# A decode layer's forward and backward pass on one core: layer norm on another engine, earlier weight loads, and a rearranged end

## The chip, the core and the metric

The kernel runs on one core of one Trainium2 chip. A core has a matmul engine (PE, with its weight loads PEld), a vector engine (DVE), a scalar engine (ACT), a general engine (POOL) and a sync engine (SP), which run their own instruction streams and wait for each other by semaphores. Sixteen DMA engines move data between the device's memory (HBM) and the on-chip memory. Matmuls write into PSUM, which has eight banks of 512 f32 columns per partition; from there ACT or DVE copy results into the on-chip memory (an "evacuation"). The metric is device time in microseconds (us) of one execution.

## The reference

The reference is a layer of a decode step with one token, for a batch of 2, and its gradients. All inputs and outputs are bf16.

```python
xn = layernorm(x)                       # x: (2, 1, 576), eps 1e-5
out = x + A(xn) + B(xn)
# A: attention over a cache
q = xn @ wq                             # wq (576, 4096): 32 heads of 128
scores = q . k * 128**-0.5              # k_cache, v_cache (2, 16, 4096, 128); 2 query heads share a kv head
p = softmax(scores);  o = p @ v
A = o @ wo                              # wo (4096, 576)
# B: a gated product
h = (xn @ w_gate) * (xn @ w_up)         # (576, 4608) each
B = h @ w_down                          # (4608, 576)
# returned: out, and by vjp with grad_out (2, 1, 576) the gradients of
# x, k_cache, v_cache, wq, wo, w_gate, w_up, w_down
```

So every cache and weight tensor is read once (92.5 MB in all), and a gradient of the same size is written (92.5 MB). Since there is one token, nearly all gradients are outer products: the gradient of K is (dscore) x (query), of V is (probability) x (output gradient), of a weight is (input) x (output gradient).

## The kernel before, in words

**Attention.** The 16 kv heads form 4 groups of 4. The main loop (L845, `for n in range(NIT)`) has 16 steps; a step handles one batch entry and two kv heads. Each step has four *slots*: two for K heads and two for V heads. `slot` loads one head (1 MB) with SP's queue (`head_load`, L520), transposes it in two halves on DVE (`head_scores`, `t32`, L121; 1.23 us each) and multiplies it with stationary rows that hold the queries or the output gradients (16 matmuls per quarter, into a one-bank PSUM tile `ps_sc`). After the two K slots `softmax` follows, after the V slots `dscores`; `contract` then multiplies K with the score gradients and V with the probabilities (64 matmuls). POOL spreads the rows into the tiles `prm` and `dsm` (`masked`), and from these the outer products for the gradients of V and K are made.

**Outer products.** `outer_units` gives 8 units for V and 8 for K per step. A unit makes 8 matmuls into `ps_o`, a PSUM tile of two banks (two such tiles exist, tag "o"), and one evacuation of 128x1024 to a bf16 tile `so`. Four units fill an `so` tile of 1 MB, and POOL's queue stores it (L585). The list `outs` holds the units; `more(2)` takes two of them at two places in a slot. `evac` chooses the engine: it keeps an account of assumed times for DVE and ACT (`load`) and gives each evacuation to the one that would be done first by the account. DVE's account also has its transposes, so ACT gets 232 of the 256 `so` evacuations.

**Gated product.** It is cut into 9 slices of 512 columns. `mlp_units` gives 8 groups per slice: `loads` (SP, into `wgu` and `wd`), then `gate_up` with `down`, `grads` with `back`, two groups for the gradient of `w_down`, two for `w_gate` and `w_up`, and `outer_tail`. The list `side` holds the groups, and `other(per)` takes `per` of them at the end of each slot, where `per` is a quarter of the list, rounded up.

**Back of a group.** `back_units` makes, when a group's eight heads are done, the output projection (`first`: 40 matmuls with `wo`, sixteen transposes into `R`, and the rows for the next step), the gradient through `wq` (`second`), and the gradients of `wo` (`outer_o`, evacuated as `sto`) and `wq` (`outer_q`, as `stq` and `stqt`). For the last group these run after the loop.

**Buffers.** Loaded tiles (`kv`, `wgu`, `wd`, `wq`, `wo`) share 12 buffers (tag "nat"); store tiles (`so`, `sto`, `stq`, ...) share 5 (tag "st"). SP's queue issues in order, so a load that waits for a buffer holds back the loads behind it.

**Start and end.** The start loads `x` and `grad_out`, makes the layer norm on DVE (L168 to L188), constant tables, and zeroed tiles on POOL (L216 to L238). The end (`final_units`) transposes the accumulated output (`output`), collects the gradient of the normalized input (`rows`) and sends it through the layer norm on DVE (`gradient`, L817 to L833).

**Order of work.** The program order in each engine is made by a scheduler from the source order, the priorities set in `Block`, and its own estimate of when operands are ready. So an instruction need not stand where the source has it.

Of the kernel before, what the change touches and what calls it, by code (L numbers as in the profile page):

```python
# [13 lines left out]
P = 128  # L14
# [9 lines left out]
def kernel(  # L24
# [55 lines left out]
    def ps_o():  # L80
        return ps.tile([P, 2, 512], FP32, tag="o", bufs=2, name="ps_o")

    class Block:

# [19 lines left out]
    def evac(out, in_, cols):  # L104
        cv = 0.16 + cols * 0.00104
        cs = 0.19 + cols * 0.00083
        if load["v"] + cv < load["s"] + cs:
            load["v"] += cv
            nc.vector.tensor_copy(out=out, in_=in_)  # L109
        else:  # L110
            load["s"] += cs
            nc.scalar.copy(out, in_)  # L112

    def dve(us):
        load["v"] += us
# [41 lines left out]
    for be in range(4):  # L157
# [9 lines left out]
    x_f = sb.tile([2, D], FP32, tag="X", bufs=3, name="x_f")  # L167
    nc.vector.tensor_copy(x_f[:], x_bf[:])  # L168

    mu = const.tile([2, 1], FP32, name="mu")  # L170
    nc.vector.reduce_sum(mu[:], x_f[:], axis=AX.X)
    nc.vector.tensor_scalar(mu[:], mu[:], 1.0 / D, None, op0=ALU.mult)
    xn_f = sb.tile([2, D], FP32, tag="nat", bufs=12, name="xn_f")
    nc.vector.tensor_scalar(xn_f[:], x_f[:], mu[:], None, op0=ALU.subtract)
    xsq = sb.tile([2, D], FP32, tag="X", bufs=3, name="xsq")
    var = const.tile([2, 1], FP32, name="var")
    nc.vector.tensor_tensor_reduce(
        out=xsq[:], in0=xn_f[:], in1=xn_f[:], scale=1.0 / D, scalar=0.0,
        op0=ALU.mult, op1=ALU.add, accum_out=var[:],
    )  # L180
    eps_t = const.tile([2, 1], FP32, name="eps_t")
    nc.vector.memset(eps_t[:], EPS)
    rstd = const.tile([2, 1], FP32, name="rstd")
    nc.scalar.activation(rstd[:], var[:], AF.Sqrt, bias=eps_t[:], scale=1.0)
    nc.vector.reciprocal(rstd[:], rstd[:])
    nc.vector.tensor_scalar(xn_f[:], xn_f[:], rstd[:], None, op0=ALU.mult)
    xn_bf = sb.tile([2, D], BF16, tag="st", bufs=5, name="xn_bf")
    nc.vector.tensor_copy(xn_bf[:], xn_f[:])  # L188

# [25 lines left out]
    Wdy = const.tile([P, NB, 2, P], BF16, name="Wdy")  # L215
    nc.gpsimd.memset(Wdy[:], 0.0)  # L216
    dyT = sb.tile([P, 2 * NB, 32], BF16, tag="X", bufs=3, name="dyT")
# [6 lines left out]
    dM = const.tile([P, 2, 2, P], BF16, name="dM")  # L224
    for t in range(2):
        nc.gpsimd.memset(W[t][:], 0.0)
    nc.gpsimd.memset(dM[:], 0.0)
    Wms = [const.tile([P, 35, 8], BF16, name=f"Wm{i}") for i in range(2)]
# [339 lines left out]
    def outer_units(rows, bd, b, l0, oview):  # L568
        m = {}

        def unit(x, ch, A):
            def f():
                if ch == 0 and A == 0:
                    m["st"] = stile([P, 4, 8, Dh], "so")
                st = m["st"]
                o = ps_o()
                with Block() as mm:
                    for c in range(4):
                        for aa in range(2):
                            a = 2 * A + aa  # L580
                            mm(o[:, aa, c * Dh:(c + 1) * Dh], lhsT=rows[32 * a:32 * a + 32, 4 * ch + c, :],
                                             rhs=bd[32 * a:32 * a + 32, x * Dh:(x + 1) * Dh], start=True, stop=True)
                evac(st[:, 2 * A:2 * A + 2, 4 * ch:4 * ch + 4, :].rearrange("p a c d -> p a (c d)"), o[:], 1024)
                if ch == 1 and A == 1:
# [56 lines left out]
    def back_units(st):  # L641
        g, wq, wo, oT = st["g"], st["wq"], st["wo"], st["oT"]
        n0 = g * GH * Dh
        m = {}

        def first():
            yp = ps_m([P, 5, 2])
            with Block() as mm:
                for dc in range(5):
                    for h in range(GH):  # L650
                        mm(yp[:, dc, :], lhsT=wo[:, h, DOFF[dc]:DOFF[dc] + P], rhs=oT[:, 0, h, 0:2],
                                         start=(h == 0), stop=(h == GH - 1))
            nc.vector.tensor_add(acc[:], acc[:], yp[:])

            rp = ps_m([P, 2, 2, P], BF16)
            for t in range(2):
                for h in range(GH):
                    a = h // 2
                    nc.tensor.transpose(rp[32 * a:32 * a + 32, t, h % 2, :], oT[:, t, h, :], ident[:])
            m["R"] = R = sb.tile([P, 2, 2, P], BF16, tag="R", bufs=1, name="R")  # L660
            nc.vector.tensor_copy(R[:], rp[:])
            rp = ps_m([P, 32, 2])
# [4 lines left out]
            m["W"] = stationaries(rp[:], lambda h: (P * h, [[1, P]]))  # L667
            dve(0.2 + 0.5)

# [3 lines left out]
        def outer_q(k, A):  # L673
            def f():
                R = m["R"]
                if A == 0:
                    m["st"] = swtile([P, 2, GH * P], "stq")
                st = m["st"]
                o = ps_o()
                with Block() as mm:  # L680
                    for dc in range(2):
                        for aa in range(2):
                            a = 2 * A + aa
                            d0 = (2 * k + dc) * P
                            mm(o[:, aa, 256 * dc:256 * dc + 256], lhsT=xnr[32 * a:32 * a + 32, d0:d0 + P],
                                             rhs=R[32 * a:32 * a + 32, 1].rearrange("p h d -> p (h d)"),
                                             start=True, stop=True)
                evac(view(st[:], 0, P, 512 * A, [[256, 2], [GH * P, 2], [1, 256]]),
                     o[:].rearrange("p a (d n) -> p a d n", d=2), 1024)
                if A == 1:  # L690
# [17 lines left out]
        def outer_o(A, h2, k):  # L708
            def f():
                R = m["R"]  # L710
                if h2 == 0 and k == 0:
                    m["so"] = swtile([P, 4, D], "sto")
                o = ps_o()
                with Block() as mm:
                    for aa in range(2):
                        a = 2 * A + aa
                        mm(o[:, aa, 0:HD2], lhsT=R[32 * a:32 * a + 32, 0, h2, :],
                                         rhs=dyr[32 * a:32 * a + 32, k * HD2:(k + 1) * HD2], start=True, stop=True)
                evac(view(m["so"][:], 0, P, h2 * D + k * HD2, [[2 * D, 2], [1, HD2]]), o[:, :, 0:HD2], D)
                if h2 == 1 and k == 1:  # L720
# [3 lines left out]

        return [[first], [second], [outer_o(0, 0, 0), outer_o(0, 0, 1)], [outer_o(0, 1, 0), outer_o(0, 1, 1)],
                [outer_o(1, 0, 0), outer_o(1, 0, 1)], [outer_o(1, 1, 0), outer_o(1, 1, 1)],
# [6 lines left out]
    def more(n):  # L733
        for _ in range(min(n, len(outs))):
            outs.pop(0)()

    def other(n):
        for _ in range(min(n, len(side))):
            for f in side.pop(0):
                f()  # L740

    def slot(src, t, b, l, s_ps, per, mid=None):
# [102 lines left out]
    for n in range(NIT):  # L845
        g, b, s = step(n)
        l0 = G * g + 2 * s
        if len(side) < 5 and nslice < NFS:
            side += mlp_units(nslice)
            nslice += 1  # L850
        per = max(1, -(-len(side) // 4))
        new = n + 1 < NIT and step(n + 1)[0] != g
# [32 lines left out]
        if new:  # L885
            st = nxt
    end_of_K(*last[:5])
    outs += outer_units(last[5], last[6], last[1], G * last[0]["g"] + 2 * last[2], okview)
    units = back_units(last[0])
    side += final[:1] + units[:2] + final[1:] + units[2:]  # L890
    while outs or side:
# [32 lines left out]
```

## Time and profile before

| | |
|---|---|
| median of 13 runs | 521.72 us (515.55 to 530.07) |
| the profiled execution | 515.92 us, span of its instructions 514.2 us |
| busy, of the span | PE 81%, PEld 65%, DVE 69%, ACT 64%, POOL 40% |
| mean granted PE clock | 0.851 of full |
| DMA | 186.26 MB, mean 362 GB/s |
| chain that ended last | PE 44%, ACT 18%, DVE 16%, DMA 10%, issue 9%, POOL 2% |
| evacuation of 128x1024 | ACT 1.02 us, DVE 1.20 us |
| DMA issue to landing, 1 MB | K 13.1 us, V 9.7 us, `so` 10.2 us (medians) |

How to read it: "busy" is the time in which an engine executed instructions; matmuls overlap, so a busy PE is not at its peak. The DMA share is the mean busy share of the sixteen DMA engines in a stretch of time; because of rounding at the packets' ends it can stand a little above 1. "Issue" in the chain is time for which the profile shows no wait. The granted clock is the share of its full clock that PE was given.

### The profile page before, as it was taken

The numbers are of one execution on the slowest core, as the hardware profiler recorded it, in microseconds if no ns is written. First come the engines' busy times: TensorE is split into PE (matmuls) and PEld (weight loads), VectorE is DVE, ScalarE is ACT, GpSimd is POOL, SyncE is SP. The second block draws the span as 40 slices with busy tenths as digits, with TensorE's granted clock in tenths as the row PEclk, the third lists the DMA queues.
The fourth block names the chain that finished last, engine by engine and source line by source line (L and its number), as shares of the span: only waits on it lengthen the run. The fifth ranks groups of instructions, "written<-read, shape, count | busy, mean of one in ns | idle before, by whom it ended". The sixth has DMA issues, their size and how long they took to land.

```text
span 514.2 us, 20063 instructions
## 1 busy us (share of the span) xinstructions
PE 416.6 (81%) x8921; PEld 332.6 (65%) x8921; DVE 356.5 (69%) x624; ACT 327.6 (64%) x454; POOL 206.2 (40%) x372
## 2 busy tenths in 40 slices
PE   1677897978897978988889879879889878799872
PEld 0576675766786756776767757757667657677630
DVE  7687866468648948376686578749694849598464
ACT  1134797658657575676576764757777656788653
POOL 6133353332632534443343525354334255453313
PEclk9989999589859778687787896979997999999655
DMA  7997999999999999999999999999999999976656
GB/s 250 398 390 293 384 383 401 391 412 400 373 400 357 348 352 416 319 408 358 353 400 327 399 416 403 373 392 418 388 417 364 420 416 396 384 280 235 249 193 237
DMA packets 52911, 186.26 MB, mean 362 GB/s; under 512 B 4140, under 2 KB 19128, under 8 KB 44632
## 3 DMA queue, kind: packets, MB, share of 16 engines
q1 hardware_dynamic: 28392, 92.49, 48.1%
q0 software_dynamic: 24432, 92.48, 45.4%
q8 instruction: 70, 1.15, 0.9%
q14 instruction: 17, 0.14, 0.1%
HBM read 92.48 MB, written 92.48 MB: 360 GB/s over the span
## 4 chain that ended last, share of the span: by engine, by line
PE 44%; ACT 18%; DVE 16%; DMA 10%; issue 9%; POOL 2%; POOLq 0%; DVEq 0%; ACTq 0%
PE ps_sc L93 16%; ACT so L112 15%; PE ps_o L93 12%; PE ps_m L93 11%; DVE X L121 5%; DMA kv<-in_A_k_cache_dram 3%; DMA out_dram<-so 3%; DVE so L109 2%; DMA wd<-in_B_w_down_dram 2%; PE ps_m L558 1%; DMA out_dram<-stqt 1%; DVE Xd L121 1%; ACT stw L112 1%; DVE Xw L121 1%; DVE stw L109 1%
## 5 line engine op out<-in xcount | busy, mean ns | idle before, releaser
L112 ACT CAST so<-ps_o 128x1024 bf16<-128x1024 f32 x232 | 225.6, 1024 | 63.3 <-PE ps_o L93 59.9
L121 DVE STREAM_TRANSPOSE X<-kv 128x1024 f32<-128x1024 f32 x128 | 157.4, 1233 | 51.7 <-PE ps_sc L93 45.9
L93 PE MATMUL ps_sc<-X,W 128*128 128x128 bf16 x2048 | 157.2, 234 | 16.1 <-issue 9.1
L93 PEld LDWEIGHTS <-W 128*128 128x128 bf16 x2048 | 139.4, 105 | 24.3 <-issue 17.6
L585 POOL DMA_DIRECT2D out_dram<-so x64 | 49.9, 780 | 121.0 <-ACT so L112 75.2
L93 PE MATMUL ps_o<-bd,dsm 32*128 32x128 bf16 x1024 | 48.4, 233 | 14.2 <-ACT so L112 8.8
L93 PE MATMUL ps_o<-bd,prm 32*128 32x128 bf16 x1024 | 45.6, 232 | 12.2 <-ACT so L112 5.0
L93 PEld LDWEIGHTS <-dsm 32*128 32x128 bf16 x1024 | 29.3, 99 | 29.0 <-issue 22.7
L93 PE MATMUL ps_m<-kv,rowT 128*32 128x128 bf16 x2048 | 43.2, 248 | 5.1 <-issue 4.3
L93 PEld LDWEIGHTS <-prm 32*128 32x128 bf16 x1024 | 27.4, 98 | 25.3 <-issue 18.4
L93 PEld LDWEIGHTS <-rowT 128*32 128x32 bf16 x2048 | 36.2, 111 | 8.1 <-issue 5.8
L112 ACT CAST stw<-ps_o 128x1024 bf16<-128x1024 f32 x28 | 28.1, 1024 | 19.6 <-PE ps_o L93 17.3
L496 POOL COPY W<-rep 32x16 bf16<-32x16 bf16 x128 | 24.9, 195 | 31.3 <-PE ps_sc L93 23.6
L564 POOL TENSOR_TENSOR prm<-pr,maskc 128x1024 bf16<-128x1024 bf16 x16 | 30.3, 1892 | 12.3 <-DVE pr L612 12.2
L564 POOL TENSOR_TENSOR dsm<-ds,maskc 128x1024 bf16<-128x1024 bf16 x16 | 30.3, 1894 | 8.5 <-DVE ds L632 8.0
L109 DVE CAST so<-ps_o 128x1024 bf16<-128x1024 f32 x24 | 28.7, 1195 | 3.3 <-PE ps_o L93 3.3
L396 POOL DMA_DIRECT2D out_dram<-stw x18 | 13.7, 759 | 34.3 <-ACT stw L112 16.5
L93 PEld LDWEIGHTS <-Wdy 128*128 128x128 bf16 x306 | 23.0, 114 | 4.6 <-POOL dM L503 3.1
L503 POOL COPY dM<-qd 128x128 bf16<-128x128 bf16 x32 | 9.2, 290 | 41.4 <-PE ps_m L509 27.5
L112 ACT CAST std<-ps_o 128x576 bf16<-128x576 f32 x36 | 22.2, 650 | 5.4 <-PE ps_o L93 4.2
L121 DVE STREAM_TRANSPOSE Xw<-wgu 128x1152 f32<-128x1152 f32 x18 | 24.4, 1361 | 1.8 <-PE ps_sc L93 1.7
L93 PEld LDWEIGHTS <-xnr 32*128 32x128 bf16 (+1 forms) x440 | 14.0, 103 | 16.7 <-issue 12.7
(172 smaller groups left out, 549.5 us busy)
## 6 DMA issues: line engine op xcount, KB each, us to landing
out_dram<-so POOLq DMA_DIRECT2D x64, 1024.0 KB, 10.2
kv<-in_A_k_cache_dram SPq DMA_DIRECT2D x32, 1024.0 KB, 13.1
kv<-in_A_v_cache_dram SPq DMA_DIRECT2D x32, 1024.0 KB, 9.7
out_dram<-stw POOLq DMA_DIRECT2D x18, 512.0 KB, 9.6
wd<-in_B_w_down_dram SPq DMA_DIRECT2D x9, 576.0 KB, 10.1
out_dram<-std POOLq DMA_DIRECT2D x9, 576.0 KB, 9.3
wo<-in_A_wo_dram SPq DMA_DIRECT2D x4, 1152.0 KB, 14.2
wgu<-in_B_w_gate_dram SPq DMA_DIRECT2D x9, 512.0 KB, 18.6
```

Source lines behind the costliest of these rows:

```text
L93: ins = nc.tensor.matmul(*args, **kwargs)
L109: nc.vector.tensor_copy(out=out, in_=in_)
L112: nc.scalar.copy(out, in_)
L121: nc.vector.transpose(out, in_)
L396: nc.gpsimd.dma_start(out[0:512, f0:f0 + FS].rearrange("(c p) n -> p c n", p=P), st[:])
L496: nc.gpsimd.tensor_copy(view(W[t][:], 32 * a, 32, 28 + 32 * a, [[2 * WW, 4], [WW + 2, 2], [1, 2]]), view(st["rep"][:], 32 * a, 32, t * 4 * ...
L503: nc.gpsimd.tensor_copy(view(dM[:], 0, P, t * 2 * P, [[P + 2, 2], [4, 32], [1, 2]]), view(st["qd"][:], 0, P, (2 if t == 0 else 1) * GH * 2 ...
L558: nc.tensor.matmul(t_ps[:], lhsT=o_sb[:], rhs=RV[:].rearrange("p x r -> p (x r)"), start=True, stop=True)
L564: nc.gpsimd.tensor_tensor(m[:], view(rows[:], 0, P, 0, [[0, 8], [1, P]]), view(maskc[:], 0, P, 0, [[1, 8], [0, P]]), ALU.mult)
L585: nc.gpsimd.dma_start(oview[b, :, :, l0 + x].rearrange("a m n -> m a n"), st[:].rearrange("p a c d -> p a (c d)"))
```

## The change

It has four parts.

1. *Layer norm.* Five passes over `x` go from DVE to ACT (`activation` with `accum_out`, bias or scale); DVE keeps the small (2x1) steps. Three memsets (`Wdy`, `dM`, `W[0]`) go from POOL to DVE.
2. *Groups per slot.* `per` becomes a third of the list instead of a quarter, and `other` ends after it has taken a `loads` group and takes nothing at the next slot. (In the step after a group's last one `per` is still set to a quarter once the back units are added.)
3. *Back units in smaller pieces.* `first` becomes `output`, `turn(0)`, `turn(1)` and `spread`; `R` is copied in two halves.
4. *End.* After the loop every third pair comes from the two one-bank `ps_sc` buffers, which the loop no longer needs, and is evacuated as two halves; the accounts of `evac` are set to zero; the last group's `stq` and `sto` tiles come from the 12 load buffers; and the order of the last groups changes: output projection, final output and half of `outer_o` come ahead of the last `end_of_K`.

```diff
+    def ps_pair():
+        pairs_made[0] += 1
+        if ending and pairs_made[0] % 3 == 0:
+            o = [ps.tile([P, 512], FP32, tag="sc", bufs=2, name="ps_x") for _ in range(2)]
+            return [t[:] for t in o], None
+        o = ps_o()
+        return [o[:, 0, :], o[:, 1, :]], o
...
+    def evac_pair(out, o, whole, cols, view_in=lambda t: t):
+        if whole is not None:
+            evac(out(None), view_in(whole[:]), cols)
+        else:
+            for a in range(2):
+                evac(out(a), view_in(o[a]), cols // 2)
...
-    nc.vector.tensor_copy(x_f[:], x_bf[:])
-    nc.vector.reduce_sum(mu[:], x_f[:], axis=AX.X)
+    nc.scalar.activation(x_f[:], x_bf[:], AF.Copy, accum_out=mu[:])
+    nc.vector.tensor_scalar(negmu[:], mu[:], -1.0 / D, None, op0=ALU.mult)
     nc.vector.tensor_scalar(mu[:], mu[:], 1.0 / D, None, op0=ALU.mult)
-    nc.vector.tensor_scalar(xn_f[:], x_f[:], mu[:], None, op0=ALU.subtract)
+    nc.scalar.activation(xn_f[:], x_f[:], AF.Identity, bias=negmu[:], scale=1.0)
-    nc.vector.tensor_tensor_reduce(
-        out=xsq[:], in0=xn_f[:], in1=xn_f[:], scale=1.0 / D, scalar=0.0,
-        op0=ALU.mult, op1=ALU.add, accum_out=var[:],
-    )
+    nc.scalar.activation(xsq[:], xn_f[:], AF.Square, accum_out=var[:])
-    nc.scalar.activation(rstd[:], var[:], AF.Sqrt, bias=eps_t[:], scale=1.0)
+    nc.scalar.activation(rstd[:], var[:], AF.Sqrt, bias=eps_t[:], scale=1.0 / D)
     nc.vector.reciprocal(rstd[:], rstd[:])
-    nc.vector.tensor_scalar(xn_f[:], xn_f[:], rstd[:], None, op0=ALU.mult)
-    nc.vector.tensor_copy(xn_bf[:], xn_f[:])
+    nc.scalar.activation(xn_bf[:], xn_f[:], AF.Copy, scale=rstd[:])
...
-    nc.gpsimd.memset(Wdy[:], 0.0)
+    nc.vector.memset(Wdy[:], 0.0)
...
-    for t in range(2):
-        nc.gpsimd.memset(W[t][:], 0.0)
-    nc.gpsimd.memset(dM[:], 0.0)
+    nc.vector.memset(dM[:], 0.0)
+    nc.vector.memset(W[0][:], 0.0)
+    nc.gpsimd.memset(W[1][:], 0.0)
...
+        stq = nat if g == NGRP - 1 else swtile
...
-                    m["st"] = swtile([P, 2, GH * P], "stq")
+                    m["st"] = stq([P, 2, GH * P], "stq")
...
     def other(n):
+        if waits[0]:
+            waits[0] -= 1
+            return
         for _ in range(min(n, len(side))):
-            for f in side.pop(0):
+            group = side.pop(0)
+            for f in group:
                 f()
+            if group[0].__name__ == "loads":
+                waits[0] = 1
+                return
...
-        per = max(1, -(-len(side) // 4))
+        per = max(1, -(-len(side) // 3))
...
+    ending.append(1)
+    load["v"] = load["s"] = 0.0
+    waits[0] = 0
+    units = back_units(last[0])
+    side += final[:1] + units[:1] + final[1:2] + units[3:5]
+    more(2)
     end_of_K(*last[:5])
     outs += outer_units(last[5], last[6], last[1], G * last[0]["g"] + 2 * last[2], okview)
-    units = back_units(last[0])
-    side += final[:1] + units[:2] + final[1:] + units[2:]
+    side += units[1:3] + final[2:] + units[5:]
     while outs or side:
         more(2)
         other(1)
```

The units of `outer_units`, `outer_q` and `outer_o` take their pair from `ps_pair` and hand it to `evac_pair`; outside the end both do what `ps_o` and `evac` did.

## The prediction

> **What bounds the kernel now.** I read three views in this order: stretches of the span (busy time of each engine, granted TensorE clock, DMA share, GB/s), then the instructions in order of time at both ends, then the chain of waits of the last 38 us.
>
> The stretches; columns are start:end, length, busy us (instructions) of PE, PEld, DVE, ACT, POOL, then clock, DMA share, GB/s:
>
> ```profile
> 10.00:40.00 30.00, 20.41 (x366) 17.92 (x367) 23.31 (x52) 8.16 (x11) 6.14 (x20) 0.94 1.04 390
> 40.00:50.00 10.00, 7.12 (x213) 6.05 (x210) 7.41 (x16) 3.49 (x8) 4.85 (x7) 1.00 0.73 277
> 50.00:450.00 400.00, 341.47 (x7414) 276.61 (x7415) 274.67 (x467) 273.64 (x382) 165.08 (x296) 0.85 1.00 386
> 450.00:476.00 26.00, 23.54 (x541) 18.79 (x538) 23.38 (x39) 22.49 (x32) 11.32 (x14) 1.00 0.68 258
> 476.00:514.20 38.20, 23.52 (x409) 12.86 (x397) 20.06 (x36) 18.25 (x22) 10.42 (x14) 0.55 0.61 225
> ```
>
> The reader is to see three regimes. From 50 to 450 us the DMA engines are full (share 1.00). At 40 to 50 they lose (1 - 0.73) x 10 = 2.7 us. From 450 on reading is over, and they run at 0.68 and 0.61: compute sets the end. No byte is added or removed by this change, so it can gain only in the gap at 40 to 50, in the last 38 us, and in what little the middle loses.
>
> The start, in order of time (start, duration, engine, instruction):
>
> ```profile
> 0.74 1.28 ACT L184 ACT_TABLE_LOAD   x1 [0.74 <-PEq L908]
> 0.94 0.19 DVE L245 MEMSET accx<- 128x160 f32 x1
> 2.07 2.79 DVE L168 CAST x_f<-x_bf 2x576 f32<-2x576 bf16 x1 [0.94 <-DMA x_bf<-in_A_x_dram]
> ...
> 8.88 0.45 DVE L188 CAST xn_bf<-xn_f 2x576 bf16<-2x576 f32 x1
> 9.26 0.21 DVE L130 CAST identf<-ident 128x128 f32<-128x128 bf16 x1
> ```
>
> The layer norm holds DVE from 2.07 to 9.33; only then come DVE's 2.3 us of constant tables, and at 12.81 the first matmul with real weights. The first cast took 2.79 us; the same cast at the end of the kernel takes 0.44.
>
> The chain that ended last, from 485 us on:
>
> ```profile
> 485.60 1.02 ACT so L112
> 486.62 0.04 issue
> 486.66 0.61 PE ps_o L93 x8
> ...
> 488.88 1.94 ACT so L112 x2
> 490.81 0.04 issue
> 490.86 1.23 PE ps_o L793 x5
> ...
> 493.73 2.29 PE ps_o L804 x8
> 496.02 0.56 PE ps_o L93 x8
> ```
>
> Matmuls and evacuations take turns: with two pairs of banks, PE waits for an evacuation, then the evacuation for PE.
>
> **Part 1, layer norm on ACT.** The nearest row for an ACT pass over 576 columns is `std`, 128x576, 0.65 us; the read of an accumulator after Exp took 0.19. From the landing at 2.07: cast with sum 0.84, `negmu` on DVE 0.14 and two hand-overs of about 0.05 (3.15), centering 0.65 (3.8), square with sum 0.84 (4.65), table load 1.28, since Sqrt now comes after another function set (5.9), Sqrt 0.29 and reciprocal 0.15 with hand-overs (6.5), scaling 0.65 (7.2). Before it was 9.33. In the built order DVE has its constants right behind the reciprocal, so they start at 6.55 instead of 9.26: 2.7 us earlier. Ahead of `negmu` stand three memsets moved from POOL, of 1152, 256 and 624 f32 elements per partition. At the rate of the `accx` row (0.19 us for 160, 0.07 for 10: 0.8 ns each) they take 1.8 us and end at 2.7, before the sum is there. At POOL's rows (2.02, 0.52 and half of 2.52) they would take 3.8 and delay it by 1.6. Behind the constants stand the `xs` copies, `dyr`, `xnr`, and the weight transposes. `wo` had landed by 11.4 (issue 3.11, 8.3 to landing), and its transpose moves only from 15.5 to 12.8.
>
> What is this worth? The DMA engines are full from 10 to 40 us on loads already issued; SP's next load stands at 46.65, waiting for a buffer. A start 2.7 us earlier frees it 2.7 earlier, and the gap has just 2.7 us to give. I take **2.5**, bounds 0 (another buffer turns out to be the late one) and 2.7.
>
> The first row above shows the table load at 1.28 us and work right after it. The Trainium skill ("ScalarE: Activation LUTs", What ACT_TABLE_LOAD costs) adds a drain of about 1.38 us to each switch, which speaks against this part: by it the start would gain 1.1. Here the load before Exp started 0.02 us after the copy ahead of it ended, so no drain stands in front of it.
>
> **Part 2, weight loads two slots ahead.** A slot is 7.1 us (16 steps of 4 slots from 24 to 478). Before, a slice's 8 groups went 2 to a slot, the loads one slot ahead. Now the first slot issues the loads alone, the second is skipped, and the rest goes 3 to a slot. DVE waited for a landing weight only here:
>
> ```profile
> DVE Xd L121 <- DMA wd<-in_B_w_down_dram: 6.7, 2, 3.5
> ```
>
> Both waits lie in stretches with a DMA share of 1.0, so removing them only makes later data late. What is new: `wgu` and `wd` hold 2 of the 12 load buffers 7.1 us longer, on SP's in-order queue the K and V loads stand behind them, and a slice's five stores come in two slots instead of four. Nothing shows a longer hold directly; the dearest row is the window 240 to 245, where loads of a new group and of a slice meet and the share is 0.58 (2.1 us lost). Bounds for 8 slices: gain 6.7, loss 8 x 2.1 = 17. I take **0**, by the 400 us row above: queued transfers cover delays of this size nearly everywhere.
>
> **Part 3, the end.** In the chain from 485 to 506 PE waits for evacuations, and for DVE steps of the final gradient ahead of them, about 11.6 us (1.0 + 1.9 + 1.0 + 1.0 for `so`, then 2.6, 0.7, 2.7 and 0.7). A third pair and both engines would hide these, bound 11.6. Less comes off. The scheduler leaves 19 units of `so` after the last score matmul instead of 16, which moves work and removes none. One pair in three is evacuated as two halves: ACT 2 x 0.58 (the `stqt` row, 512 columns) against 1.02. ACT's list from the last `bd` on sums to 23.6 us against 21.7. And `rows` moves back: the built PE order has the accx matmuls after 10 of the 16 `sto` matmuls, where before all 16 followed. On DVE the last two `stq` evacuations stand behind the whole gradient.
>
> So the end follows from this chain. PE's busy time from 476 on is 23.5 us, plus 3 units of about 0.6, of which 7.2 come from the accx matmuls on (2.29 for those, 6 `sto` at 0.21, 20 for `stq` at 0.18): 18.1 us lie ahead. The loop ends some 2.5 us sooner, as the 3 units left it. With about 3.5 us of waits left, accx starts at 473.5 + 18.1 + 3.5 = 495. The matmuls and gradient took 493.73 to 503.84 before, 7.2 without the four `sto` evacuations among them: 502.2. Two `stq` on DVE at 1.23: 504.7 instead of 508.5, and with the stores behind them about 510.2 instead of 514.2. I take **4.0**, bounds 0 (PE at half clock and the gradient chain eat it) and 11.6. The final `stq` and `sto` tiles in the load buffers, and `R` copied in halves, count as nothing: no row of the last 38 us waits for a store buffer, and `R` is 0.41 us.
>
> The row of 476 on shows the clock at 0.55; from 480 to 485 PE was busy 4.57 of 5 us and stayed at 0.50. The skill ("TensorE: Matmul & The Clock Gate", Part 1) lets the clock return after some 3.4 us of sustained work, and PE's 18.1 us would then be about 10 and the end 8 us earlier. These rows don't bear that out.
>
> **Sum.** The profiled execution took 515.92 us (span 514.2). 515.92 - 2.5 - 0 - 4.0 = 509.4. It is one of the fastest of the 13 runs shown; their median is 521.72, and the same 6.5 us off that gives **515.2**, the forecast. About 1% (5 us) is what can be told from no change.
>
> **Rivals.** (a) *The end does not shorten*, as the gradient chain and ACT's 23.6 us take the place of the bank waits: only 2.5 is left, 519.2. For it speaks that `stq` stands behind six microseconds of serial DVE work; against it, ACT was idle over half the last 38 us (18.25 busy). (b) *Slower: load buffers.* Held one slot longer, they let SP's queue run dry once per slice, and DMA idles where its share is now 1.00. At 1.9 us each (nearly the 240 us window), 8 slices cost 15.2: 521.7 - 6.5 + 15.2 = 530.4. It beats the gain from 0.8 us per slice, and makes the kernel slower by over 1% from 1.5. For it: SP waited 144 us in all for PE to free K and V buffers, 21 times. Against: DMA stayed full in spite of that. (c) *More*: all bank waits go (11.6), the gap closes (2.7) and the weight waits count for half (3.4): 504. (d) *It does nothing*: ACT's table load and the moved memsets eat the start, another load the gap, PE the end: 521.
>
> **Chances.** Forecast 0.52, (a) 0.18, (b) 0.15, (c) 0.10, (d) 0.05. The forecast's own range is 510 to 519. The range of 8 in 10 reaches halfway into (b) and (c): 505 to 527. Faster by over 1% (below 516.5) is (c), and about four fifths of the forecast's case: 0.52. Slower by over 1% is (b) and a little of (d): 0.17. Within 1%: 0.31.
>
> **What would show it.** Right: `xn_bf` ready near 7.2, first weight matmul near 10.1, share above 0.9 at 40 to 50, 50 to 450 still 1.00, and about 4 us less from the last score matmul to the end than the loop's shift explains. Wrong: DVE's memsets past 3 us; a middle share under 0.97 with SP waiting on `wd` or `wgu` readers (rival b); the last chain on DVE's gradient and `stq` with the same length (rival a); a granted clock of 1.0 in the last 30 us (rival c).

## The result

| | before | changed |
|---|---|---|
| median (runs) | 522.95 us (48) | 535.59 us (11) |
| lowest to highest | 515.11 to 531.25 | 527.13 to 537.93 |
| the profiled execution (span) | 515.92 us (514.2) | 535.76 us (533.9) |
| mean granted clock in the profile | 0.851 | 0.807 |

The ratio is 1.0218, interval [1.0158, 1.0278]: the change makes the kernel slower by 2.2%. The forecast was 515.2 us with a range of 505 to 527; the measured 535.59 us lies above it. Medians here and below are of all runs shown; the ratios leave disturbed runs out on both sides, so that a ratio can differ from the quotient of two medians.

The stretches of the changed kernel, with the columns of the prediction's first fence (start:end, length, busy us of PE, PEld, DVE, ACT, POOL, clock, DMA share, GB/s); the last two are cut at its own last score matmul:

```profile
10.00:40.00 30.00, 22.98 (x383) 20.25 (x383) 23.71 (x39) 7.72 (x11) 5.88 (x20) 0.83 1.04 386
40.00:50.00 10.00, 8.63 (x245) 7.25 (x243) 6.95 (x15) 6.37 (x13) 6.08 (x10) 1.00 1.01 380
50.00:450.00 400.00, 334.33 (x7003) 272.63 (x7001) 266.96 (x445) 259.98 (x358) 154.60 (x279) 0.81 0.95 365
450.00:492.00 42.00, 37.07 (x827) 30.77 (x827) 32.81 (x56) 32.25 (x46) 18.22 (x28) 0.92 0.82 308
492.00:533.90 41.90, 27.41 (x464) 15.66 (x461) 22.21 (x46) 22.17 (x33) 12.99 (x16) 0.58 0.61 226
```

The gap at 40 to 50 is closed (0.73 before, 1.01 now). The middle, full before, is not full any more: (1.00 - 0.95) x 400 = 20 us of DMA time are lost there. The two spans differ by 533.9 - 514.2 = 19.7 us. So between these two executions the middle accounts for the whole loss, and nothing of what start and end were to bring is left beside it. The execution of the kernel before is 7 us faster than its median, so 20 us is the difference of these two; by the ratio the change costs 2.18% of 522.95, 11.4 us. By hundreds of us from 50 on, the share is 0.94, 0.96, 0.92 and 0.98, against 1.02, 0.98, 1.00 and 1.00 before: it goes in several places, not in one.

The start, rows of ACT, DVE and PE in order of time (start, duration, engine, instruction; in brackets the idle time before it and what ended that):

```profile
2.07 0.68 ACT L190 ACTIVATE x_f<-x_bf 2x576 f32<-2x576 bf16 x1
...
2.66 0.19 ACT L190 ACTIVATION_READ_ACCUMULATOR x_f<-x_bf 2x1 f32 x1
2.98 0.08 DVE L191 TENSOR_SCALAR negmu<-mu 2x1 f32<-2x1 f32 x1
...
4.52 0.19 ACT L197 ACTIVATION_READ_ACCUMULATOR xsq<-xn_f 2x1 f32 x1
4.72 1.28 ACT L201 ACT_TABLE_LOAD   x1
6.02 0.29 ACT L201 ACTIVATE rstd<-var,eps_t 2x1 f32<-2x1 f32 x1
...
6.43 0.20 DVE L150 CAST identf<-ident 128x128 f32<-128x128 bf16 x1
6.53 0.78 ACT L204 ACTIVATE xn_bf<-xn_f,rstd 2x576 bf16<-2x576 f32 x1 [0.22 <-DVE rstd L202]
...
9.97 1.22 PE L105 MATMUL ps_m<-xs,wq 128*128 128x2 bf16 x40
```

DVE's constants start at 6.43 instead of 9.26, and the first matmul with real weights at 9.97 instead of 12.81: 2.8 us earlier.

Who held SP's queue on the `wd` load, by the waits from 50 to 450 us (engine, line, what it waited for: us in total, times, longest). The kernel before, whose `wd` load is L319, waited 4.9 us:

```profile
SPq L319 <- PE ps_m L93: 2.1, 1, 2.1
SPq L319 <- DVE Xw L121: 1.8, 1, 1.8
SPq L319 <- PE ps_o L93: 1.0, 1, 1.0
```

The changed kernel, where it is L335, waited 31.7 us:

```profile
SPq L335 <- DVE Xw L141: 13.3, 2, 7.4
SPq L335 <- PE ps_m L105: 12.3, 2, 6.6
SPq L335 <- PE ps_o L105: 3.4, 2, 2.7
SPq L335 <- DVE negb L619: 2.7, 1, 2.7
```

The K and V loads (L520 before, L536 in the changed kernel) waited longer, too, for the readers of weights, `Xw` on DVE. In both kernels they waited longest for matmuls of PE. The first two rows are of the kernel before, the last two of the changed kernel:

```profile
SPq L520 <- PE ps_o L93: 140.7, 20, 18.9
SPq L520 <- DVE Xw L121: 9.1, 2, 5.4
...
SPq L536 <- PE ps_o L105: 136.3, 23, 20.5
SPq L536 <- DVE Xw L141: 21.6, 3, 8.7
```

One case of a `wd` load that was held up, in SP's queue in order of time:

```profile
111.40 1.41 SPq L333 DMA_DIRECT2D wgu<-in_B_w_up_dram  x1
126.85 0.34 SPq L335 DMA_DIRECT2D wd<-in_B_w_down_dram  x1
132.30 0.34 SPq L536 DMA_DIRECT2D kv<-in_A_k_cache_dram  x1
147.42 1.18 SPq L536 DMA_DIRECT2D kv<-in_A_v_cache_dram  x2
```

`wd` is issued 15.5 us after `wgu`'s last load (6.6 in the same place before: 112.00 to 118.58), after waits of 7.4 us for `Xw` and 6.6 us for matmuls; the K load behind it follows at 132.30 (120.70 before) and the V loads at 147.42 (138.18 before). What had been queued lasts till about 140 (share 0.99 from 135 to 140), and then the engines run dry; stretches with the columns as above:

```profile
140.00:145.00 5.00, 3.37 (x73) 3.17 (x72) 4.74 (x9) 1.93 (x2) 1.64 (x8) 1.00 0.30 115
145.00:150.00 5.00, 4.44 (x179) 3.70 (x176) 2.13 (x5) 3.88 (x5) 3.56 (x6) 1.00 0.61 185
```

This gap belongs to part 2. Two of the runs below show it in the same stretch: e15_slots_end, which has part 2 without the halves of `R`, has it (first row), and e4_start_end, which has the halves without part 2, has not (second row):

```profile
140.00:145.00 5.00, 3.37 (x72) 3.17 (x71) 4.70 (x9) 1.90 (x2) 1.58 (x8) 0.99 0.31 117
...
140.00:145.00 5.00, 4.68 (x99) 3.92 (x102) 1.55 (x2) 1.97 (x3) 3.03 (x10) 0.52 0.99 377
```

The chain that ended last, from just ahead of the `accx` matmuls (PE L841) on (start, duration, engine, instruction; "issue" is time for which the profile shows no wait):

```profile
515.01 0.41 ACT sto L124
...
515.49 0.67 issue
516.16 0.32 POOL Wt L290
...
516.52 0.30 POOL Wt L290
...
517.97 2.31 PE ps_o L841 x8
...
522.89 0.44 DVE t L865
...
523.36 0.76 DVE t L866
...
524.14 0.53 DVE t L867
...
524.94 1.63 DVEq L962
526.58 1.14 DVE stq L121
```

From the last score matmul to the end it is 41.7 us, against 39.9 before. By the rows of PE 21 units of `so` are left then, against 18; the prediction, which counted 19 against 16, has the same three more.

### The profile page after: what moved, and what is told of

The parts are those of the page before. It is cut to its first block, busy times and chain, and to the rows that moved or that the text cites. A ratio compares the mean times of both kernels' runs of the same rounds, so it can differ in the third digit from the quotient of the medians.

```text
span 533.9 us, 20080 instructions
## 1 busy us (share of the span) xinstructions
PE 432.0 (81%) x8921; PEld 347.4 (65%) x8921; DVE 358.1 (67%) x628; ACT 334.5 (63%) x466; POOL 201.8 (38%) x369
## 4 chain that ended last, share of the span: by engine, by line
PE 43%; DVE 9%; ACT 9%; DMA 8%; issue 6%; POOL 1%; DVEq 0%; POOLq 0%; ACTq 0%
PE ps_sc L105 14%; PE ps_m L105 12%; PE ps_o L105 10%; ACT so L124 7%; DMA kv<-in_A_k_cache_dram 3%; DVE X L141 3%; DMA out_dram<-so 2%; DMA kv<-in_A_v_cache_dram 2%; DVE so L121 2%; PE ps_m L574 1%; ACT sto L124 1%; PE ps_m L646 1%; PE ps_m L624 1%; DVE Xw L141 1%; PE ps_m L525 1%
## 5 line engine op out<-in xcount | busy, mean ns | idle before, releaser
L124 ACT CAST so<-ps_o 128x1024 bf16<-128x1024 f32 x228 | 221.0, 1021 | 69.9 <-PE ps_o L105 61.6
L105 PE MATMUL ps_sc<-X,W 128*128 128x128 bf16 x2048 | 161.4, 239 | 7.6 <-DVE X L141 3.2
L105 PEld LDWEIGHTS <-W 128*128 128x128 bf16 x2048 | 144.4, 108 | 15.1 <-issue 7.7
L105 PE MATMUL ps_o<-bd,dsm 32*128 32x128 bf16 x1000 | 50.6, 247 | 20.1 <-ACT so L124 13.3
L105 PEld LDWEIGHTS <-dsm 32*128 32x128 bf16 x1024 | 33.2, 105 | 35.8 <-issue 31.3
L105 PE MATMUL ps_m<-kv,rowT 128*32 128x128 bf16 x2048 | 40.5, 239 | 5.8 <-issue 3.6
L105 PEld LDWEIGHTS <-prm 32*128 32x128 bf16 x1024 | 29.6, 98 | 21.7 <-issue 14.3
L105 PEld LDWEIGHTS <-rowT 128*32 128x32 bf16 x2048 | 34.0, 107 | 8.0 <-issue 4.1
L512 POOL COPY W<-rep 32x16 bf16<-32x16 bf16 x128 | 24.8, 194 | 22.9 <-PE ps_sc L105 15.2
L105 PEld LDWEIGHTS <-Wdy 128*128 128x128 bf16 x306 | 26.2, 124 | 4.9 <-DVE Xo L141 2.9
L105 PEld LDWEIGHTS <-xnr 32*128 32x128 bf16 (+1 forms) x440 | 12.6, 102 | 21.1 <-issue 16.4
L571 ACT COPY o_sb<-ps_m 128x128 f32<-128x128 f32 x32 | 8.7, 271 | 25.6 <-PE ps_m L105 25.5
```

The lines of the kernel that those rows point to most:

```text
L105: ins = nc.tensor.matmul(*args, **kwargs)
L512: nc.gpsimd.tensor_copy(view(W[t][:], 32 * a, 32, 28 + 32 * a, [[2 * WW, 4], [WW + 2, 2], [1, 2]]), view(st["rep"][:], 32 * a, 32, t * 4 * ...
L571: nc.scalar.copy(o_sb[:], o_ps[:])
```

## The experiments

In the expectations, "parts" are the four of the section on the change: 1 layer norm, 2 groups per slot, 3 smaller back units, 4 the end. "Hold" is worked out for each run from the profile's rows: from the issue of a slice's first `wgu` load to the end of the last DVE read of its weights (`Xw` of `wgu`; in e12_hold_tail the added read), on average over slices 2 to 9. The share is that of the DMA engines from 50 to 450 us of the profiled execution. Ratios are to the kernel before on the same chip, in the same set of runs; its median was 523.73 us beside e1, e2, e4 and e9, 522.22 beside e6, e8, e11 and e10_end_only, 525.24 beside e5, e12, e13 and e10_end_merged, 518.03 beside e15 and e16, and 525.15 beside e14 and e17. For e5 and e12 the quotient of the medians (1.035 and 1.048) is more than a percent above the ratio, so the size of these two losses is known no better than that. Share and hold are of one execution each; that of e8 took 546.02 us, 12 above its median.

| run | what it is | median us | ratio [interval] | share | hold us |
|---|---|---|---|---|---|
| before | | 522.95 | 1 | 1.00 | 43.4 |
| changed | parts 1 to 4 | 535.59 | 1.0218 [1.0158, 1.0278] | 0.95 | 49.4 |
| e1_start | part 1 | 516.51 | before: 523.73 | 0.99 | 43.3 |
| e17_start_again | part 1 | 515.37 | 0.9874 [0.981, 0.9938] | 0.98 | 42.4 |
| e2_slots | part 2 | 539.02 | 1.0324 [1.0237, 1.0411] | 0.94 | 50.1 |
| e9_ahead_even | earlier loads, even slots | 532.59 | 1.0208 [1.0126, 1.029] | 0.95 | 49.5 |
| e5_wait_only | part 2 with quarters | 543.47 | 1.0231 [1.0146, 1.0316] | 0.94 | 48.5 |
| e6_per_only | thirds only | 524.58 | 1.0105 [1.0036, 1.0173] | 0.99 | 37.1 |
| e12_hold_tail | given back later | 550.49 | 1.0371 [1.0274, 1.0469] | 0.94 | 69.5 |
| e8_before_nat11 | 11 load buffers | 534.03 | 1.0265 [1.0183, 1.0347] | 0.94 | 41.2 |
| e16_sooner | part 1, given back sooner | 523.55 | 1.0127 [1.0036, 1.0217] | 0.98 | 37.3 |
| e4_start_end | parts 1, 3, 4 | 532.93 | 1.0221 [1.0132, 1.031] | 0.96 | 45.6 |
| e10_end_only | parts 1, 4 | 517.98 | 0.9939 [0.9893, 0.9985] | 0.99 | 43.4 |
| e11_empty_group | part 1, one empty group | 516.43 | 0.9859 [0.9753, 0.9965] | 1.00 | 44.3 |
| e13_account | part 1, account + 0.1 us | 520.26 | 0.9883 [0.9789, 0.9977] | 0.98 | 43.3 |
| e10_end_merged | parts 1, 4, `R` in halves | 528.22 | 1.01 [1.0019, 1.0181] | 0.96 | 44.1 |
| e14_halves_one_tile | the same, one PSUM tile | 522.39 | before: 525.15 | 0.97 | 43.5 |
| e15_slots_end | parts 1, 2, 4 | 534.9 | 1.0336 [1.0247, 1.0426] | 0.95 | 49.1 |

### Which part costs

**e1_start** is the kernel before with part 1's hunks of the diff alone, **e2_slots** with part 2's alone, and **e4_start_end** is the changed kernel with part 2 undone, here against the changed kernel:

```diff
-        per = max(1, -(-len(side) // 3))
+        per = max(1, -(-len(side) // 4))
...
     def other(n):
-        if waits[0]:
...
         for _ in range(min(n, len(side))):
-            group = side.pop(0)
-            for f in group:
+            for f in side.pop(0):
                 f()
-            if group[0].__name__ == "loads":
-                waits[0] = 1
-                return
```

> The kernel before with part 1 alone (layer norm on ACT, three memsets on DVE). If the start gains what its trace shows (first weight matmul at 9.97 instead of 12.81 us, DMA share at 40 to 50 us 1.01 instead of 0.73), the time falls by 2 to 3 us, a ratio of 0.994 to 0.996. If the gap only moves, 1.000.

> The kernel before with part 2 alone (a third of the list per slot, loads alone in the first slot, the second skipped). Theory slots: this part alone makes the kernel slower, since the middle's DMA share fell from 1.00 to 0.95 over 400 us, 20 us: ratio 1.03 to 1.04. Rival: the end or the finer back units cost it: ratio 0.99 to 1.01, with the middle's share at 1.00.

> The kernel after with part 2 undone (a quarter of the list per slot, no skipped slot). Theory slots: faster than before, 0.985 to 0.995, by the start's 2.8 us and what the end gives (0 to 4 us), middle share 1.00. Rival: still 1.01 to 1.02, since the finer back units reorder the middle.

Part 1 gains (516.51 against 523.73 us), part 2 costs 3.2%. But parts 1, 3 and 4 without part 2 took 1.022, where a gain was expected: a second cause lies in the small pieces or the end. The two don't add up: each alone costs about as much as both (e4 has part 1's gain in it).

**e9_ahead_even** is the kernel before with a slice's `loads` issued ahead of the last groups of the slice before it, two groups to a slot and no slot skipped:

```diff
...
-            side += mlp_units(nslice)
-            nslice += 1
+            side += ready
+            ready = []
+            if nslice < NFS:
+                ready = mlp_units(nslice)
+                side.insert(len(side) - 2, ready.pop(0))
+                nslice += 1
...
```

> The kernel before with the next slice's weight loads issued two slots ahead of use, but two groups in every slot as before, none skipped. Theory crowding (three groups each in the two V slots hold up the contractions that free the K and V buffers): 0.99 to 1.01, middle share 1.00. Theory holding (weights that keep 2 of 12 load buffers longer starve the K and V loads): slower, 1.015 to 1.04, middle share 0.97 or less.

The hold goes from 43.4 to 49.5 us and the time by 2.1%, without part 2's uneven slots.

### Part 2: the hold, the thirds, or the order of the loads

**e12_hold_tail** leaves all loads where they are and has each slice's buffers given back later:

```diff
+        def hold():
+            nc.vector.tensor_tensor(held[:, 0:1], m["wd"][0:1, 0, 0:1], m["st"][0:1, 0, 256:257], ALU.mult)
+            nc.vector.tensor_tensor(held[:, 1:2], m["wgu"][0:1, 0, 0:1], m["st"][0:1, 0, 256:257], ALU.mult)
...
-                [outer_gu(0, 0), outer_gu(0, 1)], [outer_gu(1, 0), outer_gu(1, 1)], [outer_tail]]
+                [outer_gu(0, 0), outer_gu(0, 1), hold], [outer_gu(1, 0), outer_gu(1, 1)], [outer_tail]]
```

> The kernel before, where two further one-element reads on VectorE (some 0.1 us each, 16 in all) keep each slice's wgu and wd from being given back until its first stw evacuations are done, about a slot later; the order of all loads is unchanged. Theory holding (two of twelve load buffers held a slot longer cost, whichever end the slot is added to): 1.01 to 1.025, with a DMA share below 0.98 from 50 to 450. Theory order (it is the place of the weight loads in SP's queue that costs): 0.995 to 1.005.

1.037, with the order of SP's loads unchanged. The place of the loads in the queue is not needed for the loss; a longer hold alone makes one. The hold grew by 26 us here, more than the slot that was meant, and the loss is above the range that was expected. DVE itself waited only 4.2 us for the evacuations which the added reads need. The waits of SP's queue from 50 to 450 us name it:

```profile
SPq L321 <- DVE held L434: 34.2, 2, 17.8
...
SPq L526 <- DVE held L434: 20.9, 1, 20.9
```

`wd` (L321) and K or V loads (L526) wait 55 us for the added one-element reads.

**e5_wait_only** and **e6_per_only** take part 2 apart: the first has its new `other` and keeps `// 4`, the second has only

```diff
-        per = max(1, -(-len(side) // 4))
+        per = max(1, -(-len(side) // 3))
```

> The kernel before, with the loads alone in their slot and the next slot skipped, but still a quarter of the groups to a slot: part 2 without its third. Part 2 whole took 1.032, the third alone 1.0105. Theory holding: 1.015 to 1.025, the larger share of part 2. Theory crowding (three groups to a slot after a skipped one): 1.00 to 1.01.

> The kernel before with a third of the waiting groups in each slot instead of a quarter; loads and first uses stay in one slot, and weights are given back about a slot sooner, in more crowded slots. Theory holding (the hold of load buffers decides): not slower, 0.98 to 1.00. Theory crowding (more side work in a slot delays the K and V reads that free buffers): 1.01 to 1.03.

By the ratios the wait alone costs 2.3% and the thirds alone 1.05%, together about the 3.2% of part 2; by the medians it is 3.5% and 0.5% against 2.9%. So the wait is the larger share, as theory holding has it, but how the loss divides isn't settled. In e6 the hold is shorter than before (37.1 us) and the kernel is no faster: this loss, at the lower end of what theory crowding expected, is not one of hold. The middle is nearly full (0.99), and 2 us of some 5 (by the ratio) lie at the start: the share at 40 to 50 us is 0.53 there, against 0.73. Where the rest lies isn't shown.

**e8_before_nat11** prices a buffer: `bufs=12` becomes `bufs=11` for tag "nat".

> The kernel before with 11 load buffers instead of 12, nothing else. If load buffers bound the stream, a slice's two buffers held one slot longer are about 2 x 7 us x 8 slices of buffer time out of 12 x 430, 2.2% of it; one buffer less is 8.3%, so it should cost over three times as much as the even loads two slots ahead (1.021): 1.05 to 1.09. If the order of the requests matters and the number of buffers does not: 0.99 to 1.02.

2.7%, less than the 5 to 9% expected. So the loss does not grow in proportion to buffer time: 6 us more of hold (e9) cost nearly as much as a whole buffer, and 26 us (e12) cost one and a half to two times as much as a buffer (3.7% by the ratio, 4.8% by the medians). That buffers bound the stream is confirmed; the linear price behind the expectation is not.

**e16_sooner** goes the other way, on top of part 1:

```diff
     def other(n):
-        for _ in range(min(n, len(side))):
-            for f in side.pop(0):
+        while n > 0 and side:
+            group = side.pop(0)
+            for f in group:
                 f()
+            if group[0].__name__ != "loads":
+                n -= 1
```

> Part 1, and the loads of a slice not counted as one of the two groups of their slot, so that the gradients that read the weights last come in the same slot as the loads: the hold of wgu, 43 us on average over slices 2 to 9 in part 1 alone, gets shorter by half a slot or more. Theory holding, taken to the other side: 0.97 to 0.985 against 0.987 for part 1. If a full DMA queue can't be filled further and crowding costs: 0.99 to 1.01.

The hold is 37.3 us and nothing is gained: 1.013, against 0.987 for part 1 alone, and above both expected ranges. The share from 50 to 450 is 0.98, as in part 1 alone, and at 40 to 50 it is 0.58, where part 1 alone has 0.99 (e17): 4 us of a loss of some 13. The middle was full, so a shorter hold had little to gain there. That the crowded slots cost the rest is argued, not shown.

### Parts 3 and 4: the end, the groups, or the halves

**e10_end_only** is part 1 with the new end, where the loop's groups keep the old units:

```diff
+        if g < NGRP - 1:
+            return [[first], [second], [outer_o(0, 0, 0), outer_o(0, 0, 1)], [outer_o(0, 1, 0), outer_o(0, 1, 1)],
...
         return [[output, lambda: turn(0)], [lambda: turn(1), spread], [second], [outer_o(0, 0, 0), outer_o(0, 0, 1)], [outer_o(0, 1, 0), outer_o(0, 1, 1)],
```

**e11_empty_group** is part 1 with ten groups as the changed kernel has them, but no instruction changed:

```diff
-                        side[0:0] = back_units(last[0])
+                        back = back_units(last[0])
+                        side[0:0] = back[:1] + [[lambda: None]] + back[1:]
```

> Part 1 and the new ending (third pair, new order of the last units, stores in the load buffers), with the loop's groups and slots as before: TensorE's order is that of part 1 alone until the last stretch. Part 1 alone took 0.986 of before (516.5 us), and parts 1, 3 and 4 together 1.022. Theory loop (the loss of parts 3 and 4 arises inside the loop, from the finer back units, and the ending itself moves nothing): 0.98 to 0.99, and from the last K load to the end 95 to 98 us. Theory end (the ending itself costs): 1.00 or more, the last stretch longer than 99 us. The prediction's step of 4 us for the end: 0.978, the last stretch near 93.

> Part 1, and one empty group behind the first back unit, so that a group's back work is 10 groups of units as in the changed kernel; no instruction is added or removed, but the following units, weight loads among them, move by up to a slot. Theory phase (it is the count of groups that costs, as it decides in which slot later units fall): slower than part 1 alone by over 1.5%, so 1.00 to 1.03. Theory instructions (the finer units themselves, R in halves and the extra bank turns cost): as part 1 alone, 0.98 to 0.99.

The end gives nothing: 0.994 with it, 0.987 without (intervals overlap, so whether it costs is open). From the last K load to the end it takes 99.6 us here, as theory end has it, against 96.8 and 97.8 in the two profiles of part 1 alone (e1, e17), 93.3 in e11 and 99.1 in the kernel before; the ratio lies between the ranges of the two theories. The count of groups alone costs nothing either (0.986), although it changes the order of TensorE's work in many places. **e13_account** shifts evacuations between the engines in another way, and that is harmless as well (0.988):

```diff
-            dve(0.2 + 0.5)
+            dve(0.2 + 0.6)
```

> Part 1, with the planner's account for VectorE raised by 0.1 us per group, as the halves of R raise it; the same instructions, but some evacuations may go to the other engine. Theory halves: as part 1 alone, 0.98 to 0.99. If any small shift in the order of evacuations costs 2 to 3%: 1.00 to 1.02.

So not every small shift of order costs 2%, and e4's loss needs a cause of its own. **e10_end_merged** has the small units, but in nine groups as before (against e4_start_end):

```diff
-                        side[0:0] = back_units(last[0])
+                        back = back_units(last[0])
+                        side[0:0] = [back[0] + back[1]] + back[2:]
```

> As the kernel with part 1 and the new ending (0.994), but in the loop, too, R is turned and copied in halves out of two small PSUM tiles; the four small units stand in one group, so that a group's back work is 9 groups as before. Theory halves (the further ps_m tile, with its hand-over from TensorE to VectorE and back in the middle of a slot, costs): 1.015 to 1.025, as parts 1, 3 and 4 together (1.022), with TensorE standing several us in a piece behind VectorE. Theory groups (only the halves and ten groups together cost): 0.99 to 1.00.

1.010 against 0.994 for the same without the halves, and the intervals don't overlap: in the loop the halves of `R` cost 1.6%, less than theory halves expected and more than its rival. The mechanism expected for it is hardly seen: TensorE's longest wait for DVE from 50 to 450 us is 4.1 us, once. **e14_halves_one_tile** turns both halves into one PSUM tile and leaves the copies in two pieces:

```diff
-            rp = ps_m([P, 2, P], BF16)
+            if g == NGRP - 1:
+                rp = ps_m([P, 2, P], BF16)
+            else:
+                if t == 0:
+                    m["rp"] = ps_m([P, 2, 2, P], BF16)
+                rp = m["rp"][:, t]
...
```

> As the kernel with R in halves in nine groups (1.010), but in the loop both halves are turned into one PSUM tile, as before, and only the copies stay halved; TensorE's order stays nearly the same, sixteen score matmuls between the halves. Theory tile (the further ps_m tile costs): 0.99 to 1.00. Theory order (the turns and copies in two pieces cost, wherever they land): 1.005 to 1.015.

522.39 us against 525.15 is 0.995 by the medians, as theory tile has it, but there is no interval, and the runs lie between 516.42 and 527.21. So the further PSUM tile is a candidate for the loss, and why the halves cost stays open.

One event of e4 shows how a small delay grows. TensorE, with the idle time ahead of the instruction and what ended it in brackets:

```profile
248.63 0.37 PE L617 MATMUL ps_m<-one,mr 1*128 1x1 f32 x1 [11.88 <-DVE mr L615]
```

DVE in the same time:

```profile
240.10 0.24 DVE L613 TENSOR_REDUCE m<-ps_m 1x4 f32<-1x128 f32 x1
247.10 1.38 DVE L141 STREAM_TRANSPOSE Xd<-wd 128x1152 f32<-128x1152 f32 x1 [6.76 <-DMA wd<-in_B_w_down_dram]
248.40 0.17 DVE L615 COPY mr<-m 1x128 f32<-1x128 f32 x1
```

And SP's queue:

```profile
234.51 0.55 SPq L335 DMA_DIRECT2D wd<-in_B_w_down_dram  x1
235.15 0.44 SPq L536 DMA_DIRECT2D kv<-in_A_k_cache_dram  x1
256.22 0.81 SPq L536 DMA_DIRECT2D kv<-in_A_v_cache_dram  x2
```

`wd` lands 12.6 us after its issue. Its transpose stands on DVE ahead of the small copy `mr`, which softmax needs; so DVE waits, TensorE stands 11.9 us, the heads in the buffers are not finished, and SP's next load comes only at 256.22. The DMA share from 250 to 260 is 0.28. This is the landing wait that part 2 takes away; the changed kernel has no wait of DVE for a landing weight. It pays for that with the hold.

**e15_slots_end** undoes the halves in the changed kernel itself, with the same lines as e10_end_only.

> The changed kernel with R turned whole again in the loop (the finer units only for the last group): parts 1, 2 and the new ending. Part 2 alone took 1.032, part 1 and the ending 0.994; in the changed kernel (1.022) the halves come on top. If the two causes add: 1.005 to 1.01, as the halves took 1.6% elsewhere. If the longer hold alone sets the pace and the halves hide behind it: 1.015 to 1.03.

1.034 without the halves, 1.022 with them, and above both expected ranges: where the hold is long, the halves cost nothing more. The intervals overlap, so a gain from them isn't shown. This makes the two causes plain. Undoing part 2 alone (e4, 1.022) or the halves alone (e15, 1.034) leaves the kernel slow; undoing both (e10_end_only, 0.994) leaves no loss. And e15 is e10_end_only with part 2 put in: 1.034 against 0.994, intervals far apart, so in this surrounding part 2 costs 4%.

**e17_start_again** is e1_start once more, with six runs.

> Part 1 alone once more, for its interval. The prediction's step of 2.5 us: 0.995, bounds 0.9948 to 1.000. By the medians of the first look (516.5 against 523.7): 0.986.

0.9874 [0.981, 0.9938]. Part 1 alone beats both kernels, with about 515 to 517 us; no version here is clearly faster than it.

## Why the prediction was wrong

**Start, -2.5 us: right in its mechanism, too small.** Constants came 2.83 us earlier (2.7 was worked out), the first weight matmul 2.84 us, the share at 40 to 50 is 1.01, and SP's K load after the gap moved from 46.6 to 43.7 us. The memsets on DVE kept `negmu` waiting for hardly anything: the sum was there at 2.85 and `negmu` ran at 2.98. Alone the part is worth 1.3% by the ratio, 6.6 us with an interval of 3.2 to 9.9, more than the upper bound of 2.7. The bound was the gap in one profiled execution, which with 515.92 us was 7 us under the median of its kernel; where a usual execution gains the rest isn't shown.

The prediction gave the drain that the Trainium skill ("ScalarE: Activation LUTs", What ACT_TABLE_LOAD costs) states for a table switch, about 1.38 us, and held two rows of the kernel before against it. One of them it misread: its first row shows no work right after the load, since ACT's next work, Sqrt, stood waiting for `var` till 7.54. The changed kernel decides it against the drain: the read of the sum of squares ends at 4.71, the load starts at 4.72 and takes 1.28, and Sqrt starts at 6.02.

**Part 2, 0 us: the step that failed.** Its sentence was "queued transfers cover delays of this size nearly everywhere". The 400 us row with a share of 1.00 was read as a reserve. It is none: SP waited in that stretch again and again for buffers (140.7 us of the K and V loads' waits are put down to matmuls into `ps_o` alone), so a load held up on SP's in-order queue has only as much cover as is already in flight. In the changed kernel SP stands 31.7 us before `wd` loads instead of 4.9, and the DMA engines lose 20 us from 50 to 450. Where the sum has 0, part 2 alone costs 3.24% (e2_slots), 17 us with an interval of 12 to 22. That this is the prediction's bound on the loss side, 17, is luck: the bound took 2.1 us per slice from one window of the kernel before, where two kinds of load meet, and nothing there shows a longer hold.

The size of the hold was off as well. The text has the loads "one slot ahead" before and two after. By the rows, on average over slices 2 to 9, `Xd` read `wd` 16.8 us after its issue before and 35.1 us in the changed kernel: 18 us later, not 7.1. The hold of `wgu` rose by only 6.0 us; why by no more isn't shown (without the thirds, in e5, it is 48.5 us).

**End, -4.0 us: it didn't come.** The prediction's path from the last score matmul was 495 - (474.3 - 2.5) = 23.2 us to the `accx` matmuls and 510.2 - 495 = 15.2 from there on. It took 25.8 (492.2 to 517.97) and 15.9, in all 41.7 instead of 38.4. In the first stretch the chain still runs over evacuations in spite of the third pair: ACT `so` 1.02 twice, DVE `so` 0.69 and 1.24, the copies of the output row, and at the last POOL's `Wt`, for which the `accx` sums wait and which the prediction had not on its path. PE stood 2.4 us for `Wt` and 0.8 us for `accx`, more than the 2.6 us by which this stretch came out too long. In the second the gradient and `stq` stand as it said. So rival (a)'s sign came: the last chain runs over DVE's gradient and `stq`, and the stretch is no shorter.

The bound of 11.6 us was too large as well. It added up evacuations and gradient steps on the chain as if PE stood for all of them; by PE's own waits it stood 5.3 us from 485 to 506, as matmuls into the other pair ran meanwhile. From the last score matmul to the end PE waited 9.1 us before and 8.1 us in the changed kernel: the waits moved, the longest now being for `stq` (2.5) and `Wt` (2.4). The sum slips a little, too: 508.5 - 504.7 is 3.8, not 4.0.

**`R` in halves, costed at nothing: wrong in the loop.** It was weighed only for the last 38 us. In the loop it costs 1.6% where loads are not held longer (e10_end_merged against e10_end_only), while no cost shows in the changed kernel (e15). Why it costs in the loop stays open.

**Rivals.** (b) came true, with the sign that was named for it: a middle share of 0.95 and SP waiting on the readers of weights (`Xw`: 34.9 us for K, V and `wd` loads together, against 10.9 before). The sign alone doesn't prove it, since e4 has a share of 0.96 with a hold of 45.6 us; e2 and e15 do. It names only one of the two causes. It was put at 15.2 us and 530.4; the result is 535.6, as the middle lost 20 between the two profiles and the end gave nothing. Its chance of 0.15 was argued down with "DMA stayed full in spite of that", the same reading of the 1.00 row.

## What to carry to other kernels

A DMA share of 1.00 leaves little to gain there, as in e16; it doesn't say that there is slack. Where the load queue waits for buffers all the time, earlier loading means longer holding, and it has to be priced as buffers taken away: look for who waits on the queue's head, not for who waits on the data. Before a slot or an order is changed, move only that: here part 1 and part 2 could be built alone, parts 3 and 4 on top of part 1, and only part 1 gained.

## What the runs showed of the hardware

**The clock and the time go together.** Over 57 runs of the kernel before on the chips of these experiments, the mean granted TensorE clock lay between 0.791 and 0.864, and the time fell by 2.2 us per 0.01 of clock (correlation -0.76). The changed kernel's median clock is 0.807 against 0.829. One piece of work shows it: the contraction of a V head took 1.08 us at 136.76 in e10_end_only, and in e10_end_merged, in the same order of work, 1.90 us at 140.37. The stretch 130 to 145, e10_end_only:

```profile
130.00:145.00 15.00, 12.99 (x326) 11.23 (x324) 8.11 (x17) 9.31 (x13) 8.35 (x18) 0.87 0.84 326
```

and e10_end_merged:

```profile
130.00:145.00 15.00, 14.40 (x242) 12.79 (x240) 7.46 (x17) 7.22 (x10) 8.58 (x16) 0.50 0.67 249
```

TensorE is the busier one, at a clock of 0.50, and the DMA share is lower. What sets the clock, and whether a low clock is cause or consequence of the stalls, was not tried. It isn't needed for the loss: e9_ahead_even, with a median clock of 0.837, is 2.1% slower than the kernel before, which had 0.833 beside it.

**Losses did not add.** Part 2 costs 3.2% and parts 3 and 4 some 3.5% over part 1 (1.0221 against 0.9874); all together end at 1.022, 3.5% over part 1. One explanation would be that both starve the same queue of buffers, so that the slack which one cause makes covers the other. e4 and e15 fit it, but no run tests it.
